# Turned keys and queries fetched chunk by chunk, and running sums of logs placed directly ahead of or within the second chunk's value products

## The chip, the cores and the metric

The kernel runs on one core of one Trainium2 chip. The metric is the device time of that core in microseconds; less is better. The engines that matter here are TensorE (PE: matrix products, results in PSUM), VectorE (DVE), ScalarE (ACT) and SyncE (SP), which issues most of the DMAs. Each engine executes its own instructions strictly in the order in which they stand in its program.

## The reference

Attention with a complex gate, followed by a two-layer MLP whose activation is h·cos(h). B=4 sequences, H=8 heads, S=768 steps, D=48; the MLP is 384 → 2048 → 384 on 3072 tokens. All in float32.

```python
mag = np.sqrt(a_re * a_re + a_im * a_im)
scale = np.minimum(mag, 0.999) / (mag + 1e-06)
a_re_n, a_im_n = (a_re * scale, a_im * scale)
for t in range(S):
    new_re = ar * S_re - ai * S_im          # ar, ai: step t of the gate
    new_im = ar * S_im + ai * S_re
    S_re, S_im = (new_re + outer(k[t], v[t]), new_im)
    y[:, :, t] = q[t] @ S_re
...
x = y.transpose(0, 2, 1, 3).reshape(B * S, H * D)
h = x @ w_in
out = (h * np.cos(h)) @ w_out
```

The kernel doesn't step through t. Since the gate multiplies, the state at step t is a sum over earlier steps s with weight P(t)/P(s), where P is the running product of the complex gate. So keys are divided by P and queries multiplied by it (written as real vectors of 96 = 2 x 48 numbers), and within a chunk of steps the result is a masked matrix product. The running product comes from logs: its magnitude is the exponential of a running sum of the log of the magnitude, its phase a running sum of angles.

## The kernel before

**Tiling.** The 3072 (sequence, step) rows are cut into 24 chunks of 128 steps, six to a sequence. Two chunks make a group; there are 12 groups, 0 to 11. The main loop runs over groups 2 to 11; below, **pass n** is its turn for group n. Groups 0 and 1 go through a start-up part ahead of it.

**What a pass does.** Pass n carries three groups at once:

- Group n, attention. For each of its two chunks: `sc` (scores, `f_scores`, L1021: 8 heads, keys `kT` against queries `qT`, in two halves of four heads), which DVE masks into `atm`; `sp` (`state_sums`, L1090, called by `f_state`: keys `ks` against values `v`, what the chunk adds to the running state; it is left out in the last chunk of a sequence, which is the second chunk of passes 2, 5, 8 and 11); `yp` (value products, `f_out`, L1036: four pairs of heads, p = 0 to 3, each with two products of `atm` with `v` and two of `qT` with `state`). ACT copies `yp` to `yT` (two copies for each chunk). "First scores" and "second scores" of a chunk pair are those of its first and its second chunk. After both chunks `yT` is sent to DRAM as `x` (`f_x`, L1118) and fetched back in another layout as `xT` (`f_xt`, L1127).
- Group n, first layer. `xT` times `w_in` gives `hp` (part of the columns by three products of split numbers: `xx`, `xh`, `xl`, the cross product being `hb`); `gate` is `hp` times its cosine. Group n-1, second layer: seven products of blocks, `sum` and `op`, with `t_...` and `w_out` against sums of `gate`; their result `ot` goes out. These fill PE between the steps of attention.
- Group n+1, the gate. ACT and DVE work out the log of the magnitude, `lg`, and split it into two halves, `hi` (ACT, L733) and `lo` (DVE). PE sums them along the steps: `lgs` (`p_powers`, L822: for each of two chunks one product with `hi` and one with `lo`, four matmuls in all, in two PSUM tiles). ACT takes four exponentials of `lgs` (P and 1/P), loads another table, and takes the arctangent of the angle. The angle is split and summed in the same way: `phs` (`g_phase`, L928). Sine and cosine of that, times P, turn keys and queries (`ks`, `qs`, `g_stack`, L963). DVE then transposes them in 32x32 blocks (`tr`, in `f_transpose`, L978), SP sends them to a DRAM buffer `moved` (one for keys, one for queries), and fetches them from there as `kT` and `qT`, with 96 numbers on the partitions and the steps along the free axis, as `sc` of the next pass wants them.

The tiles `kT` and `qT` exist once each, and so does `yT`. PSUM tiles of `sc`, `sp`, `yp`, `lgs` and `phs` come from one pool of five buffers (`pa`).

**What sets the order.** The body of a pass is one call of `weave`. It takes lists of steps, each with two numbers lo and hi between 0 and 1, spreads a list's steps evenly from lo to hi, sorts all by position, and calls them. For PE that order is final. So it is for the DMAs on SP's queue: `behind` adds an order without a wait between two of them. DVE and ACT are ordered by a scheduler that looks at what each step depends on. The row that matters here is `(prods(n + 1), 0.2285, 0.2315)`: the two `p_powers` calls of the next group, at those positions. `(chunks(n), 0.0, 0.36)` holds, for chunk after chunk, two calls of `f_scores`, `f_state` and `f_out`.

```python
def prods(g):                                              # L1458
    return powers(g) if 0 <= g < NG else []
...
for n in range(g * G, g * G + G):                          # L1483, chunks(g)
    for hh in range(2):
        yield lambda n=n, hh=hh: f_scores(n, hh)
    yield lambda n=n: f_state(n)
    yield lambda n=n: f_out(n)
```

**The fetch of turned keys and queries.** In the main loop `f_transpose` is called with both chunks at once, first for `kT`, then for `qT`. The call for `kT` only sends. The call for `qT` sends the queries and then issues four key fetches, one for each quarter of the steps of a chunk (q4, 32 steps), each with both chunks and all heads, and then two query fetches, one for each chunk. The loads and stores that `turned_first` and `rest_of` (L1501, L1506) put on the queue come behind the last query fetch.

Of the kernel before, what the change touches and what calls it, by code (L numbers as in the profile page):

```python
# [487 lines left out]
def fast_path(ctx, tc, q, k, v, a_re, a_im, moe_w_in, moe_w_out, out, least, odd, wide,  # L488
# [7 lines left out]
    nc = tc.nc  # L496
    B, H, S, D = q.shape
    DM, DF = moe_w_in.shape
    C = 128
    NCH = S // C  # L500
    G = 2
# [5 lines left out]
    Q4 = C // 32  # L507
# [26 lines left out]
    late = {}  # L534
# [8 lines left out]
    def behind(ins, other):  # L543
        tc.add_manual_dep(ins.ins, other.ins.name, mybir.DependencyInfo(
            mybir.DependencyClass.NoSync, mybir.DependencyReason.DATA))
# [14 lines left out]
    X = [dict() for _ in range(NG)]  # L560
# [130 lines left out]
    def matmul(out, **kw):  # L691
        chain(nc.tensor.matmul(out, **kw), "tensor")  # L692
# [193 lines left out]
    def p_even(g, i, n):  # L886
        for _ in even_steps(g, i, n):
            pass
# [10 lines left out]
    def p_apply(g, i, n):  # L899
        x = X[g]  # L900
        P, Q, u = (cut(x[name], i, n) for name in ("P", "Q", "mag"))
        x["applied"] = vector.tensor_tensor(out=Q, in0=cut(x["k"], i, n), in1=Q, op=ALU.mult)
        if g > PEG:
            return lambda: vector.tensor_tensor(out=u, in0=cut(x["q"], i, n), in1=P, op=ALU.mult)
        vector.tensor_tensor(out=u, in0=cut(x["q"], i, n), in1=P, op=ALU.mult)

    def g_angle(g, i, n):

        at = cut(X[g]["tan"], i, n)
        special(out=at, in_=at, func=AF.Arctan)  # L910
# [4 lines left out]
    def g_carry(g):  # L915

        n, some = g * G, ds(C - 32, 32)
        if g >= PEG and n % NCH:
            head = cut(X[g]["tan"], 0, 1)[some]
            X[g]["carried"] = vector.scalar_tensor_tensor(  # L920
                out=head, in0=before(n)[some], scalar=carry[some], in1=head,
                op0=ALU.mult, op1=ALU.add)

    def g_split(g):
        if g >= PEG:
            X[g]["split"] = upper_half(g, cut(X[g]["tan"], 0, G), 1.0 / math.pi)()
# [51 lines left out]
    def f_transpose(g, i, n, name):  # L978


        tr = ft.tile([C, NB, n * H, 32], F32, tag=name, name="tr", bufs=1)
        turn = vector.transpose(out=tr, in_=X[g][name[0] + "s"][:, ds(i * H, n * H)].rearrange(
            "p x a d -> p x (a d)").rearrange("p x (r b) -> p b x r", b=NB))
        X[g][name + " turn"] = turn
        if g and name == AHEAD and "apart" in X[g - 1]:
            behind(turn, X[g - 1]["apart"])
        elif g and "apart" in X[g - 1]:
            behind(turn, X[g - 1]["product"])
        moved = rows_d.tile([Q4, D2, n * H, 32], F32, tag="moved", name="moved", bufs=3)
        put = nc.sync.dma_start(out=moved.rearrange("q (r b) x j -> (q r) b x j", b=NB), in_=tr)  # L990
        behind(put, late.get("ends", late["x"]))
        X[g][name] = ft.tile([D2, G * H, Q4, 32] if name == "kT" else [D2, G, Q4, H, 32], F32,
                             tag=name, name=name, bufs=1)
        if name == "kT":
            X[g]["moved keys"] = moved
        else:
            for q4 in range(Q4):
                behind(nc.sync.dma_start(out=X[g]["kT"][:, ds(i * H, n * H), q4],
                                         in_=X[g]["moved keys"][q4]), put)
            for i_ in range(n):  # L1000
                late["qT"] = nc.sync.dma_start(
                    out=X[g][name][:, i_], in_=moved[:, :, ds(i_ * H, H)].rearrange("q c x j -> c q x j"))

    def f_turn(g, i, name, hh):

# [9 lines left out]
    def queries(n, h):  # L1015
        g, i = divmod(n, G)
        if g < PEG:
            return X[g]["qT"][:, i * H + h].rearrange("p q j -> p (q j)")
        return X[g]["qT"][:, i, :, h]
# [13 lines left out]
        if "whole" in X[n // G - 1]:  # L1033
            behind(y["masked"], X[n // G - 1]["whole"])

    def f_out(n):  # L1036
        y, (g, i) = Y[n], divmod(n, G)
        vals = X[g]["v"][:, i]
        state = y.get("state")
        if i == 0:  # L1040
            X[g]["yT"] = ft.tile([C, HH, G, C], F32, tag="yT", name="yT", bufs=1)
        ps = pa.tile([C, HH, C], F32, tag="a", name="yp")
        for p in range(HH):
            for side in range(2):
                matmul(ps[ds(side * 64, D), p], lhsT=vals[:, 2 * p + side],
                       rhs=y["atm"][:, 2 * p + side], start=True, stop=(state is None))
            if state is not None:
                for side in range(2):
                    matmul(ps[ds(side * 64, D), p], lhsT=state[:, 2 * p + side],
                           rhs=queries(n, 2 * p + side), start=False, stop=True)  # L1050
        for side in range(2):
            half = ds(side * 64, D)
            copied = scalar.copy(out=X[g]["yT"][half, :, i], in_=ps[half])
            if g >= PEG:
                behind(copied, late["upper"])
# [399 lines left out]
    def powers(g):  # L1455
        return [lambda i=i: p_powers(g, i) for i in range(G)]

    def prods(g):  # L1458
        return powers(g) if 0 <= g < NG else []

    def carries(g):
        if not 0 <= g < NG:
            return
        yield lambda: g_angle(g, 0, G)
        if g <= PEG:
            yield lambda: (g_carry(g), g_split(g))
            yield lambda: (p_even(g, 0, G), p_apply(g, 0, G))
        else:
            yield lambda: p_around(g)
# [4 lines left out]
    def angles(g):  # L1474
        if g < NG:
            yield lambda: g_rest(g)
        if g + 1 < NG:
            yield lambda: load(g + 1, ("re",))
# [4 lines left out]
    def chunks(g):  # L1483
        for n in range(g * G, g * G + G):
            for hh in range(2):
                yield lambda n=n, hh=hh: f_scores(n, hh)
            yield lambda n=n: f_state(n)
            yield lambda n=n: f_out(n)
        yield lambda: (f_x(g), g + 2 < NG and load(g + 2, ("im",), put=after_x), f_xt(g))
        if PEG < g + 1 < NG:  # L1490
            yield lambda: (ends(g + 1), load(g + 1, ("v",), put=lambda **kw: behind(
                nc.sync.dma_start(**kw), late["ends"])))
        if g + 2 < NG:
            late["next"] = [lambda: load(g + 2, ("k", "q"), put=turned_first)]
# [23 lines left out]
    def second(g, i):  # L1518
        return [lambda j0=j0: mm2(g, i, j0, 4) for j0 in range(0, NJ, 4)] if g < PLAIN else []
# [289 lines left out]
    for n in range(2, NG):  # L1809
        turned_keys, plain = list(keys(n + 1)), n == PLAIN  # L1810
        split = x_halves(n) if any(three(n, jp) for jp in THREE) else ()
        guard_ = list(guarded(("kT", "qT"))) if n > 2 else []
        convert = [lambda jp=jp: halves(jp) for jp in THREE if FROM[jp] == n + 1]
        weave((mixes(n - 1, 2, 4), 0.0, 0.08), (logs(n + 1), 0.0, 0.02), (chunks(n), 0.0, 0.36),
              (upper[2:] if plain else [], 0.0, 0.2), (products(n - 1, 0, 1), -0.02, -0.01),
              (products(n - 1, 1, 2), 0.05, 0.24), (products(n - 1, 2, 3) if n < NG - 1 else [], 0.28, 0.36),
              (mixes_again(n - 1, "s3"), 0.06, 0.18), (mixes_again(n - 1, "s2"), 0.19, 0.27),
              (angles(n + 1), 0.2695, 0.2699), (prods(n + 1), 0.2285, 0.2315), (carries(n + 1), 0.336, 0.34), (second(n - 1, 1), 0.36, 0.5),
              (mixes_again(n - 1, "s4"), 0.37, 0.48),
              (products(n - 1, 2 + (n < NG - 1), 7), 0.4, 0.56),  # L1820
              (convert[0:-2], 0.76, 0.76), (convert[-2:], 0.76, 0.98),
              (phases(n + 1), *((0.472, 0.476) if plain else (0.476, 0.484))),
              (turned_keys[0:1], 0.5, 0.5), (split[0:1], *[0.54 if n < NG - 1 else 0.525] * 2), (turned_keys[1:2], 0.53, 0.53),
              (turned_keys[2:3], 0.56, 0.56), (turned_keys[3:4], 0.6, 0.6), ([lambda: rest_of(n - 1)], 0.605, 0.605), (split[1:2], *[0.542 if n < NG - 1 else 0.53] * 2),
              (split[2:3], *[0.544 if n < NG - 1 else 0.54] * 2), ([lambda: p_end(n + 1, 0, G)] if n + 1 < NG else [], 0.615, 0.615), (last_quarter() if plain else [], 0.9, 1.0), (first(n), 0.56, 1.0),
              (mixes(n, 0, 2), 0.98 if convert else 0.92, 1.0 if n < NG - 1 else 0.97), (guard_[0:1], 0.47, 0.47),
              (guard_[1:2], 0.505, 0.505))
# [102 lines left out]
```

## Time and profile before

| | us |
|---|---|
| three timed runs | 638.99, 636.96, 638.65 |
| median | 638.65 |
| the profiled execution | 638.96 |
| its span | 637.2 |

The profile describes one execution. Busy time of an engine is the sum of its instructions; the groups of instructions that the profile lists by line, engine and tile show what it was spent on. The five costliest groups on PE are `hp` from `xT` (104.8 us in 492 matmuls), `op` (102.9 in 464), `hp` from `xh` (60.2 in 342) and from `xl` (59.0 in 342), and `sum` (52.5 in 304). `sc` takes 50.0 us in 384; the heaviest group of ACT is `gate` from `hp` (67.2 us in 96), that of DVE `gate` from `hp` (39.1 in 57). A float32 matmul stands as two records in the trace, so the 8 products of `sp` are 16 there.

Most matmuls have the same line, 692, a helper through which all of them go; they are told apart by their tiles, written out<-in. A line also shows the number of records (x16) and, in square brackets, what the first of them waited for: the time, the engine and tile that released it. SPq is the DMA queue of SP: a row there is a DMA being issued, not its transfer.

The granted clock of PE was 0.997 of full speed over the span, and the DMA queues moved 94.97 MB in it.

### The profile page before, as it was taken

The page shows a single profiled execution, that of the slowest core. Times are in us where ns is not written, and L with a number is a line of the kernel's source. Part 1 is how long each engine was busy: PE and PEld are TensorE (multiplying, and loading weights), DVE is VectorE, ACT ScalarE, POOL GpSimd, SP SyncE. Part 2 cuts the span into 40 slices and gives each one's busy share as a digit, 9 for nine tenths or more (in the row PEclk, how much of TensorE's full clock was granted, in tenths as well). Part 3 has the DMA queues.
Part 4 walks back from the last instruction along what each step waited for, and adds up shares of the span by engine and source line. Part 5 has one row for each costly group of instructions (what it writes and reads, how often), then busy time and mean ns, then how long its engine had stood idle before and what let it go on. Part 6 is the DMA issues. An engine that isn't in the chain of part 4 may idle for free.

```text
span 637.2 us, 11706 instructions
## 1 busy us (share of the span) xinstructions
PE 618.9 (97%) x4417; PEld 569.8 (89%) x4417; DVE 543.8 (85%) x878; ACT 463.0 (73%) x832; POOL 28.5 (4%) x45
## 2 busy tenths in 40 slices
PE   8999999999999999999999999999999999999996
PEld 5788868677889989998999999999999999989996
DVE  6999989888898798899999999989989989983471
ACT  7888687294697596698698697598598598661450
POOL 4010110000000000000000000000000000000000
PEclk9999999999999998999999999999999999999999
DMA  9968564725926647476486486496496494371001
GB/s 235 242 193 224 182 188 82 204 53 113 248 65 159 167 109 198 133 166 174 136 189 173 125 200 168 107 223 170 115 214 170 103 224 126 99 174 50 26 2 32
DMA packets 236926, 94.97 MB, mean 149 GB/s; under 512 B 208862, under 2 KB 229087, under 8 KB 236859
## 3 DMA queue, kind: packets, MB, share of 16 engines
q1 hardware_dynamic: 229320, 68.51, 46.1%
q0 software_dynamic: 5824, 25.50, 12.5%
q8 instruction: 37, 0.61, 0.4%
q10 hardware_dynamic: 1714, 0.11, 0.2%
q14 instruction: 31, 0.25, 0.1%
HBM read 69.28 MB, written 24.81 MB: 148 GB/s over the span
## 4 chain that ended last, share of the span: by engine, by line
PE 70%; ACT 14%; DVE 8%; DMA 4%; issue 3%; SPq 0%; ACTq 0%; DVEq 0%
PE hp L692 20%; PE op L692 16%; PE sum L692 13%; PE yp L692 5%; PE sc L692 5%; PE sp L692 3%; PE hb L692 3%; DMA qT<-moved 3%; PE phs L692 2%; ACT xT L681 2%; ACT gate L712 2%; DVE tr L681 2%; ACT rs L712 1%; DVE ks L681 1%; ACT tan L712 1%
## 5 line engine op out<-in xcount | busy, mean ns | idle before, releaser
L692 PE MATMUL hp<-xT,w_in 128*128 128x256 f32 (+1 forms) x492 | 104.8, 369 | 0.0
L692 PE MATMUL op<-w_out,gate 128*128 128x192 f32 (+1 forms) x464 | 102.9, 372 | 0.0
L692 PEld LDWEIGHTS hp<-xT,w_in 128*128 128x128 f32 x492 | 89.7, 190 | 12.6 <-issue 0.2
L712 ACT ACTIVATE gate<-hp,half_pi_b 128x512 f32<-128x512 f32 x96 | 67.2, 701 | 41.1 <-PE hp L692 22.4
L692 PEld LDWEIGHTS op<-w_out,gate 128*128 128x128 f32 x464 | 78.7, 190 | 15.2 <-issue 0.4
L692 PE MATMUL hp<-xh,wh 128*128 128x256 f32 x342 | 60.2, 285 | 0.0
L692 PE MATMUL hp<-xl,wl 128*128 128x256 f32 x342 | 59.0, 281 | 0.0
L681 ACT ACTIVATE xT<-hp 128x512 bf16<-128x512 f32 x96 | 58.5, 609 | 0.0
L692 PE MATMUL sc<-qT,kT 96*128 96x128 f32 x384 | 50.0, 279 | 2.6 <-DMA qT<-moved 2.3
L692 PEld LDWEIGHTS sc<-qT,kT 96*128 96x128 f32 x384 | 46.4, 191 | 6.8 <-issue 4.2
L692 PE MATMUL sum<-w_out,gate 128*128 128x192 f32 x304 | 52.5, 326 | 0.0
L692 PEld LDWEIGHTS hp<-xh,wh 128*128 128x128 f32 x342 | 48.9, 188 | 1.5 <-ACT xh L681 1.4
L692 PEld LDWEIGHTS sum<-w_out,gate 128*128 128x128 f32 x304 | 49.5, 190 | 0.1
L692 PE MATMUL hb<-xx,wx 128*128 128x256 f32 x342 | 48.6, 282 | 0.0
L692 PEld LDWEIGHTS hp<-xl,wl 128*128 128x128 f32 x342 | 48.4, 188 | 0.0
L681 DVE SCALAR_TENSOR_TENSOR gate<-hp,gate 128x512 f32<-128x512 f32 x57 | 39.1, 685 | 9.9 <-ACT xT L681 9.9
L681 ACT ACTIVATE gate<-hb 128x512 f32<-128x512 f32 x57 | 35.7, 626 | 13.0 <-PE hb L692 11.9
L681 DVE TENSOR_TENSOR hp<-hp,gate 128x512 f32<-128x512 f32 x57 | 39.2, 693 | 6.7 <-PE hp L692 2.6
L692 PEld LDWEIGHTS hb<-xx,wx 128*128 128x128 f32 x342 | 44.0, 188 | 0.0
L681 ACT ACTIVATE ot<-sum 128x192 f32<-128x192 f32 x39 | 12.8, 329 | 38.4 <-PE sum L692 35.6
L681 DVE TENSOR_TENSOR atm<-sc,causal 128x512 f32<-128x512 f32 x48 | 32.2, 682 | 7.3 <-PE sc L692 6.9
L681 ACT COPY yT<-yp 48x512 f32<-48x512 f32 x44 | 25.4, 577 | 17.0 <-PE yp L692 16.3
(162 smaller groups left out, 1286.0 us busy)
## 6 DMA issues: line engine op xcount, KB each, us to landing
moved<-tr SPq DMA_DIRECT2D x20, 768.0 KB
raw<-in_moe_w_in_dram POOLq DMA_DIRECT2D x16, 768.0 KB, 6.1
raw<-in_moe_w_out_dram POOLq DMA_DIRECT2D x16, 768.0 KB, 5.2
kT<-moved SPq DMA_DIRECT2D x40, 192.0 KB
qT<-moved SPq DMA_DIRECT2D x20, 384.0 KB
k<-in_k_dram SPq DMA_DIRECT2D x24, 192.0 KB
q<-in_q_dram SPq DMA_DIRECT2D x24, 192.0 KB
v<-in_v_dram SPq DMA_DIRECT2D x24, 192.0 KB
```

The source lines that it names most:

```text
L681: ins = getattr(self.engine, op)(**kw)
L692: chain(nc.tensor.matmul(out, **kw), "tensor")
L712: chain(nc.scalar.activation(func=func, **kw))
```

## The change

It has two parts.

**The fetch.** In place of four key fetches with both chunks and then two query fetches, it is now, for the first chunk, four key fetches of half the size and the query fetch of that chunk, and then the same for the second chunk. Each is ordered behind the one ahead of it. The bytes are the same; the number of DMAs in a pass goes from six to ten.

**The sums of logs.** `prods(n + 1)` leaves the table of the pass. `f_out` gets a function `between` and calls it ahead of its first pair of heads, or ahead of its third (p = 2) in the last chunk of a sequence. `chunks` passes `prods(g + 1)` in for the second chunk of a group.

```diff
--- before.py
+++ after.py
@@ -994,12 +994,15 @@
         if name == "kT":
             X[g]["moved keys"] = moved
         else:
-            for q4 in range(Q4):
-                behind(nc.sync.dma_start(out=X[g]["kT"][:, ds(i * H, n * H), q4],
-                                         in_=X[g]["moved keys"][q4]), put)
             for i_ in range(n):
-                late["qT"] = nc.sync.dma_start(
-                    out=X[g][name][:, i_], in_=moved[:, :, ds(i_ * H, H)].rearrange("q c x j -> c q x j"))
+                part = ds(i_ * H, H)
+                for q4 in range(Q4):
+                    home = nc.sync.dma_start(out=X[g]["kT"][:, part, q4],
+                                             in_=X[g]["moved keys"][q4, :, part])
+                    behind(home, put)
+                put = late["qT"] = nc.sync.dma_start(
+                    out=X[g][name][:, i_], in_=moved[:, :, part].rearrange("q c x j -> c q x j"))
+                behind(put, home)
 
     def f_turn(g, i, name, hh):
 
@@ -1033,7 +1036,7 @@
         if "whole" in X[n // G - 1]:
             behind(y["masked"], X[n // G - 1]["whole"])
 
-    def f_out(n):
+    def f_out(n, between=lambda: None):
         y, (g, i) = Y[n], divmod(n, G)
         vals = X[g]["v"][:, i]
         state = y.get("state")
@@ -1041,6 +1044,8 @@
             X[g]["yT"] = ft.tile([C, HH, G, C], F32, tag="yT", name="yT", bufs=1)
         ps = pa.tile([C, HH, C], F32, tag="a", name="yp")
         for p in range(HH):
+            if p == (0 if n % NCH < NCH - 1 else 2):
+                between()
             for side in range(2):
                 matmul(ps[ds(side * 64, D), p], lhsT=vals[:, 2 * p + side],
                        rhs=y["atm"][:, 2 * p + side], start=True, stop=(state is None))
@@ -1485,7 +1490,7 @@
             for hh in range(2):
                 yield lambda n=n, hh=hh: f_scores(n, hh)
             yield lambda n=n: f_state(n)
-            yield lambda n=n: f_out(n)
+            yield lambda n=n: f_out(n, lambda: n % G and [t() for t in prods(g + 1)])
         yield lambda: (f_x(g), g + 2 < NG and load(g + 2, ("im",), put=after_x), f_xt(g))
         if PEG < g + 1 < NG:
             yield lambda: (ends(g + 1), load(g + 1, ("v",), put=lambda **kw: behind(
@@ -1815,7 +1820,7 @@
               (upper[2:] if plain else [], 0.0, 0.2), (products(n - 1, 0, 1), -0.02, -0.01),
               (products(n - 1, 1, 2), 0.05, 0.24), (products(n - 1, 2, 3) if n < NG - 1 else [], 0.28, 0.36),
               (mixes_again(n - 1, "s3"), 0.06, 0.18), (mixes_again(n - 1, "s2"), 0.19, 0.27),
-              (angles(n + 1), 0.2695, 0.2699), (prods(n + 1), 0.2285, 0.2315), (carries(n + 1), 0.336, 0.34), (second(n - 1, 1), 0.36, 0.5),
+              (angles(n + 1), 0.2695, 0.2699), (carries(n + 1), 0.336, 0.34), (second(n - 1, 1), 0.36, 0.5),
               (mixes_again(n - 1, "s4"), 0.37, 0.48),
               (products(n - 1, 2 + (n < NG - 1), 7), 0.4, 0.56),
               (convert[0:-2], 0.76, 0.76), (convert[-2:], 0.76, 0.98),
```

What the change moves on PE, in pass 3, where the second chunk isn't the last of its sequence. The rows start at the second half of the second scores; a row is a line, an operation, out<-in, the shape of one and how many in a row. Before:

```order
L692 MATMUL sc<-qT,kT 128x128 x4
L692 MATMUL lgs<-hi,exact 128x384
L692 MATMUL lgs<-lo,exact 128x384
L692 MATMUL lgs<-hi,exact 128x384
L692 MATMUL lgs<-lo,exact 128x384
L692 MATMUL sp<-v,ks 96x48 x8
L692 MATMUL yp<-atm,v 48x128 x2
```

PE in pass 3 after the change:

```order
L692 MATMUL sc<-qT,kT 128x128 x4
L692 MATMUL sp<-v,ks 96x48 x8
L692 MATMUL lgs<-hi,exact 128x384
L692 MATMUL lgs<-lo,exact 128x384
L692 MATMUL lgs<-hi,exact 128x384
L692 MATMUL lgs<-lo,exact 128x384
L692 MATMUL yp<-atm,v 48x128 x2
```

The four sums have gone behind the eight products of `sp`; the rest of these rows stands as it did.

PE in pass 5, where the second chunk is the last of its sequence and has no `sp`. Before:

```order
L692 MATMUL sc<-qT,kT 128x128 x4
L692 MATMUL lgs<-hi,exact 128x384
L692 MATMUL lgs<-lo,exact 128x384
L692 MATMUL lgs<-hi,exact 128x384
L692 MATMUL lgs<-lo,exact 128x384
L692 MATMUL yp<-atm,v 48x128 x2
L692 MATMUL yp<-qT,state 48x128 x2
L692 MATMUL yp<-atm,v 48x128 x2
L692 MATMUL yp<-qT,state 48x128 x2
L692 MATMUL yp<-atm,v 48x128 x2
```

PE in pass 5 after the change:

```order
L692 MATMUL sc<-qT,kT 128x128 x4
L692 MATMUL yp<-atm,v 48x128 x2
L692 MATMUL yp<-qT,state 48x128 x2
L692 MATMUL yp<-atm,v 48x128 x2
L692 MATMUL yp<-qT,state 48x128 x2
L692 MATMUL lgs<-hi,exact 128x384
L692 MATMUL lgs<-lo,exact 128x384
L692 MATMUL lgs<-hi,exact 128x384
L692 MATMUL lgs<-lo,exact 128x384
L692 MATMUL yp<-atm,v 48x128 x2
```

Here the sums have gone behind the first two pairs of heads of `yp`. The other passes are as one of these two: 4, 6, 7, 9 and 10 as pass 3, 2 and 8 as pass 5; pass 11 has no next group and no sums.

SP's queue at the place in a pass where the turned queries are sent and fetched (`tr` is the transposed tile, `moved` the DRAM buffer, `ot` a result of the second layer). Before:

```order
L990 DMA moved<-tr 128x1536 x2
L998 DMA kT<-moved 96x16x32 x4
L1001 DMA qT<-moved 96x4x256 x2
L1502 DMA out_dram<-ot 128x384 x2
```

SP's queue at the same place after the change (the new lines shift the numbers: L998 is L1000, L1001 is L1003, L1502 is L1507):

```order
L990 DMA moved<-tr 128x1536 x2
L1000 DMA kT<-moved 96x8x32 x4
L1003 DMA qT<-moved 96x4x256
L1000 DMA kT<-moved 96x8x32 x4
L1003 DMA qT<-moved 96x4x256
L1507 DMA out_dram<-ot 128x384 x2
```

The first chunk's queries stand ahead of the second chunk's keys, and the stores behind have four more DMAs ahead of them. On ACT the order is the same, but that a table load stands behind the two copies of `yT` in passes 2 and 8, where it stood ahead of them. On DVE a few steps of the state and of the end of the running product change places with steps of the gate, and the transposing of the queries stands one or two gate steps later in one or two passes.

## Prediction

> **What bounds the kernel now.** The page comes first: its busy times and the shares of the chain that ended last.
>
> ```profile
> span 637.2 us, 11706 instructions
> PE 618.9 (97%) x4417; PEld 569.8 (89%) x4417; DVE 543.8 (85%) x878; ACT 463.0 (73%) x832; POOL 28.5 (4%) x45
> PE 70%; ACT 14%; DVE 8%; DMA 4%; issue 3%; SPq 0%; ACTq 0%; DVEq 0%
> ```
>
> TensorE (PE) works 97% of the span and carries 70% of the chain. VectorE (DVE), the next engine, has 15% of room. So a change that adds and removes no arithmetic can only gain where PE stands still, and the second view is the list of what PE waited for.
>
> ```profile
> PE lgs L692 <- DVE lo L681: 3.0, 5, 0.8
> PE sc L692 <- DMA qT<-moved: 2.3, 3, 1.5
> PE lgs L692 <- ACT hi L733: 2.0, 4, 0.8
> ```
>
> The columns are total us, times, longest. These are the three largest waits of the main loop. Two of them belong to the running sums of logs (`lgs`, 5.0 us in nine waits), one to the scores (`sc`) at the head of a pass, which wait for turned keys and queries (2.3 us in three). The change touches these two places and no other.
>
> The timeline of PE gives the true price of a wait. A row reads start, length, line, out<-in, count of weight loads and matmuls. First pass 7, where `lgs` waits for nothing, then pass 6, where it waits twice.
>
> ```profile
> 385.79 1.06 PE L692 MATMUL sc<-qT,kT 96*128 96x128 f32 x8
> 386.60 0.42 PE L692 MATMUL lgs<-hi,exact 128*128 128x384 f32 x1
> 386.86 0.34 PE L692 MATMUL lgs<-lo,exact 128*128 128x384 f32 x1
> 387.38 1.48 PE L692 MATMUL sp<-v,ks 128*96 128x48 f32 x16
> 388.79 0.43 PE L692 MATMUL yp<-atm,v 128*48 128x128 f32 x4
> 390.69 0.59 PE L692 MATMUL sum<-t_s,gate 128*128 128x192 f32 x2
> ```
> ```profile
> 335.64 1.06 PE L692 MATMUL sc<-qT,kT 96*128 96x128 f32 x8
> 336.91 0.44 PE L692 MATMUL lgs<-hi,exact 128*128 128x384 f32 x1 [0.21 <-ACT hi L733]
> 337.90 0.45 PE L692 MATMUL lgs<-lo,exact 128*128 128x384 f32 x1 [0.56 <-DVE lo L681]
> 338.54 1.48 PE L692 MATMUL sp<-v,ks 128*96 128x48 f32 x16
> ```
>
> From the start of the second scores to the start of `sp` pass 7 takes 387.38 - 385.79 = 1.59 us, pass 6 takes 338.54 - 335.64 = 2.90. The two waits cost 1.31 us, while the brackets add up to 0.77: each break in the stream costs 0.27 more than its bracket. For nine waits that is 5.0 + 9 x 0.27 = **7.4 us**.
>
> **The change, part one: what stands in front of `lgs`.** Nothing is added or removed; four `lgs` matmuls move behind `sp`, or in the last chunk of a sequence behind half of `yp`. From pass 7: `sp` lasts 388.79 - 387.38 = 1.41 us, `yp` 390.69 - 388.79 = 1.90, so half of it 0.95, and `lgs` starts 0.81 after the second scores. In passes 6 and 9 `sp` covers the whole wait: in pass 6 `lgs` would start at 335.64 + 0.81 + 1.41 = 337.86; its second matmul comes 386.86 - 386.60 = 0.26 later and finds `lo` there (337.90). In passes 3, 4 and 5 something stays:
>
> ```profile
> 184.24 1.06 PE L692 MATMUL sc<-qT,kT 96*128 96x128 f32 x8
> 186.95 0.45 PE L692 MATMUL lgs<-lo,exact 128*128 128x384 f32 x1 [0.83 <-DVE lo L681]
> ...
> 235.75 1.06 PE L692 MATMUL sc<-qT,kT 96*128 96x128 f32 x8
> 238.57 0.44 PE L692 MATMUL lgs<-lo,exact 128*128 128x384 f32 x1 [0.56 <-DVE lo L681]
> ...
> 288.08 1.06 PE L692 MATMUL sc<-qT,kT 96*128 96x128 f32 x8
> 290.74 0.45 PE L692 MATMUL lgs<-lo,exact 128*128 128x384 f32 x1 [0.55 <-DVE lo L681]
> ```
>
> Pass 3 would ask for `lo` at 184.24 + 0.81 + 1.41 + 0.26 = 186.72 and gets it at 186.95; pass 4 at 238.23 and 238.57; pass 5, with only 0.95 in front, at 290.10 and 290.74. With 0.27 for each break that leaves 0.5 + 0.6 + 0.9 = 2.0 us. **Part one is worth 7.4 - 2.0 = 5.4 us.** Its ends: 7.4 if all of it were covered; 0 if the sums turn out to wait as long behind `sp`, for a PSUM bank that ACT has to empty first.
>
> What is moved late by this: in passes 7, 8 and 10, which wait for nothing today, the sums come 0.95 to 1.41 us later, and with them four exponentials, a table load and the copies of `yT` on ACT, then the way of `x` through DRAM to the first `hp`.
>
> ```profile
> 388.89 1.28 ACT L708 ACT_TABLE_LOAD   x1
> 390.81 0.58 ACT L681 COPY yT<-yp 48x512 f32<-48x512 f32 x1 [0.64 <-PE yp L692]
> ...
> 301.86 0.38 SPq L1132 DMA_DIRECT2D xT<-x  x1
> ...
> 307.51 1.67 PE L692 MATMUL hp<-xT,w_in 128*128 128x256 f32 x7
> ...
> 586.15 0.38 SPq L1132 DMA_DIRECT2D xT<-x  x1
> ...
> 589.48 0.56 DVE L681 TENSOR_SCALAR cut<-xT 128x768 uint32<-128x768 uint32 x1 [1.28 <-DMA xT<-x]
> ```
>
> In pass 7 the table load ends 0.64 before `yp` is done; 1.41 later it would hold `yT` up by 0.77. The last row pair says that `xT` is there 589.48 - 586.15 = 3.3 us after its issue (DVE was waiting for it), and the pass with the least room, pass 5, has 307.51 - 301.86 = 5.65. So 2.3 us of cover lie over 0.77, or over the 0.8 by which PE gets ahead in pass 5. I count this delay at nothing; without that cover it costs 0.8 us in each of nine passes, 7 us.
>
> **Part two: keys and queries chunk by chunk.** The same bytes in 8 key transfers of half size instead of 4, and the first chunk's queries after four of them. The case that waits longest is pass 11.
>
> ```profile
> 325.17 2.76 PE L692 MATMUL sum<-w_out,gate 128*128 128x192 f32 x16
> 327.77 1.50 PE L692 MATMUL sc<-qT,kT 96*128 96x128 f32 x12
> ...
> 566.36 2.76 PE L692 MATMUL sum<-w_out,gate 128*128 128x192 f32 x16
> 570.63 2.02 PE L692 MATMUL sc<-qT,kT 96*128 96x128 f32 x16 [1.51 <-DMA qT<-moved]
> 577.10 1.16 PE L692 MATMUL sc<-qT,kT 96*128 96x128 f32 x8
> ```
> ```profile
> 557.91 6.31 SPq L998 DMA_DIRECT2D kT<-moved  x4
> 564.40 1.68 SPq L1001 DMA_DIRECT2D qT<-moved  x2
> ```
> ```profile
> L998 SPq DMA_DIRECT2D kT<-moved x40: 584/1260/3012, 114.0 to 563.4; - x40
> ```
>
> Pass 6 shows the pace without a wait: scores 2.60 us after the last `sum`. Pass 11 takes 4.27, so its wait costs 1.67, or 0.16 more than its bracket. For three waits: 2.3 + 3 x 0.16 = **2.8 us**.
>
> Do these go? A key transfer holds the queue for 0.58 to 3.0 us at one size (last row, least, median, most), so most of that is waiting for room and should follow the amount. The trace has no half transfer. Bounds: half the pass-11 mean, 0.79, or all of it, 1.58. I take 0.79, since 0.58 without a jam for a whole one lies below it. Then the first chunk is issued by 557.91 + 4 x 0.79 + 0.84 = 561.9 instead of 565.2, and if it lands 5.4 us later as now (570.63 - 565.24), at 567.3, before PE wants it at 566.36 + 2.60 = 568.96. Even 1.2 us each would do. The second chunk's issue ends where it does now and is wanted at 577.10 - 1.67 = 575.4. The stores and loads behind it on the queue keep their time, and above 0.79 wait with it. **Part two: 2.8 us; ends 0 and 3.1** (a few tenths in passes 8 and 10 are not in the list).
>
> **A third term: the clock.** In pass 4 the granted clock falls to half right after the two `lgs` waits.
>
> ```profile
> 239.20 1.76 PE L692 MATMUL sp<-v,ks 128*96 128x48 f32 x16
> ...
> 244.10 2.87 PE L692 MATMUL sum<-t_s,gate 128*128 128x192 f32 x16
> ```
> ```profile
> 241.00:243.00 2.00, 2.00 (x20) 1.98 (x22) 2.00 (x4) 1.49 (x2) 0.00 (x0) 0.50 0.92 224
> ```
>
> The third number from the right is the clock: 0.50. From `sp` to `sum` pass 4 takes 4.90 us, pass 7 390.69 - 387.38 = 3.31: the stretch costs **1.6 us**. It is the only one in the loop, and it begins some 2 us after PE stood for 239.20 - 235.75 - 1.59 = 1.86 us at the two sums. Of the three timed runs one is 1.7 to 2.0 us below the others, which looks like a run without it. With two thirds of that wait gone (0.6 stays) I expect the stretch gone too.
>
> The Trainium skill, "TensorE: Matmul & The Clock Gate", part 1, puts the fall to half clock behind at least one idle window of about 3.4 us. No gap here is that long, so by that rule these waits do not cause the stretch, and it would stay; the trace, with half clock after shorter gaps, does not bear the rule out, but it is one event.
>
> **The sum.** The profiled execution took 638.96 us (span 637.2 and 1.76 around it), 0.3 above the median of 638.65. 638.96 - 5.4 - 2.8 - 1.6 = **629.2 us**.
>
> **Rivals.** *The clock stretch stays, or falls elsewhere*: 638.96 - 8.2 = 630.8. For it: a single event in the loop, not seen after the 1.3 us of pass 6.
>
> *Part two brings nothing*, since the first chunk lands no earlier: half transfers at over 1.2 us. 638.96 - 5.4 - 1.6 = 632.0. Against it: 0.58 for a whole one.
>
> *The late exponentials hold up `xT`*, without the cover: 629.2 + 7 = 636. Against it: the 2.3 us; part of it is likelier than all.
>
> *Slower: a transfer has a price of its own.* If a half key transfer holds the queue as long as a whole one, 1.58, the second chunk of pass 11 is issued by 557.91 + 8 x 1.58 + 1.68 = 572.2 and lands at 577.6, 2.2 after PE wants it. In nine passes that is 20 us, with part two lost: 638.96 + 20 - 7.0 = 652. It decides from (575.4 - 5.4 - 1.68 - 557.91) / 8 = 1.3 us each. For it: the median of 1.26 is near. Against it: the least of 0.58.
>
> The Trainium skill, "DMA: Bandwidth & Descriptors", anatomy of one DMA, gives every transfer about 2.0 us fixed plus bytes / 436e3, and its rules tell authors to merge small ones; four more transfers in series would be an estimated 8 us later. The trace has whole ones at a mean of 1.58, below that fixed part alone, so they overlap.
>
> *Waits only move*, to `lo` of the phase sums or a gate: about 638, for no row shows where.
>
> **How the numbers follow.** Forecast 0.42, clock stays 0.20, part two nothing 0.12, `xT` 0.12, slower 0.06, waits only move 0.08. A measurement here tells some 0.3%, 1.9 us, from no change. Faster: the first three and most of the fourth, 0.83; same 0.11; slower 0.06. Range: low end with all of part one, 3.1 and the clock, 638.96 - 12.1 = 626.9; the high end takes in 632.0 and the milder part of the `xT` case, 635.5.
>
> **What would show it.** PE's list of waits: no `sc` behind `qT`, `lgs` at 1 us or so, in three passes. The key rows of the queue: near 0.8 us each, 6.3 for eight. The clock at 1.00 from 238 to 246. Wrong would be: `hp` or `phs` in that list, second scores waiting for `qT`, or `lgs` waiting as long as before.

## The result and the profile after

| | before | after |
|---|---|---|
| four timed runs, median | 637.81 us (636.74 to 638.99) | 631.48 us (631.48 to 631.77) |
| ratio | | 0.9902, 95% interval 0.9879 to 0.9924 |
| profiled execution | 638.96 us, span 637.2 | 631.48 us, span 629.6 |

The change makes the kernel faster by 1.0%. In the experiments below two runs stand far outside all others (2387.1 and 1059.3 us) and are left out of the counts; they move a median by less than 0.1 us. Execution against execution that is 7.5 us, where the forecast had 9.8. The page of the changed kernel, its busy times and its chain:

```profile
span 629.6 us, 11793 instructions
PE 617.2 (98%) x4417; PEld 567.4 (90%) x4417; DVE 542.8 (86%) x878; ACT 462.9 (74%) x832; POOL 28.6 (5%) x45
PE 87%; ACT 6%; DVE 2%; DMA 2%; SPq 1%; issue 1%; ACTq 0%; DVEq 0%
```

PE now carries 87% of the chain instead of 70. PE's list of waits in the main loop:

```profile
PE sum L692 <- ACT ot L681: 1.4, 2, 1.1
PE yp L692 <- DVE atm L681: 0.3, 1, 0.3
PE lgs L692 <- DVE lo L681: 0.2, 1, 0.2
```

All three waits of before are gone or nearly so (2.3 us behind `qT`, 5.0 us at `lgs`). A new one has come, and it is the largest: a sum of the second layer behind ScalarE's copy `ot`.

The list doesn't say what this is worth. That comes from the starts of rows in PE's timeline, pass by pass, in us. A is from the first scores to the last start in the second chunk's `yp`, B from there to `phs`, C from the last `sum` to the next pass's scores.

| pass | A before | A after | B before | B after | C before | C after |
|---|---|---|---|---|---|---|
| 2 | 14.52 | 14.86 | 7.87 | 7.87 | 2.60 | 2.60 |
| 3 | 14.20 | 12.89 | 8.09 | 8.08 | 2.59 | 2.60 |
| 4 | 16.79 | 13.87 | 8.09 | 9.48 | 2.60 | 2.60 |
| 5 | 13.72 | 12.98 | 8.09 | 8.59 | 2.60 | 2.60 |
| 6 | 13.75 | 12.53 | 8.09 | 8.33 | 3.30 | 2.60 |
| 7 | 13.42 | 13.42 | 8.09 | 8.08 | 2.73 | 2.60 |
| 8 | 12.10 | 12.36 | 8.09 | 8.09 | 3.00 | 2.60 |
| 9 | 13.35 | 12.52 | 8.09 | 8.34 | 2.83 | 2.60 |
| 10 | 13.41 | 13.41 | 8.09 | 8.09 | 4.27 | 2.60 |

C gives back 3.13 us: the scores wait nowhere. A gives back 1.31, 0.74, 1.22 and 0.83 in passes 3, 5, 6 and 9, and 2.92 in pass 4, of which some 1.6 is the stretch of half clock. Against that stand two losses: 0.34 and 0.26 in A of passes 2 and 8, where the sums now break the value products, and 1.39 + 0.50 + 0.24 + 0.25 = 2.4 us in B of passes 4, 5, 6 and 9.

Pass 4 shows where B's loss comes from. First come rows of PE in the changed kernel (start, length, line, out<-in, records, and in brackets the wait), then rows of ScalarE from the same stretch.

```profile
235.52 1.48 PE L692 MATMUL sp<-v,ks 128*96 128x48 f32 x16
236.82 0.42 PE L692 MATMUL lgs<-hi,exact 128*128 128x384 f32 x1
237.42 0.44 PE L692 MATMUL lgs<-lo,exact 128*128 128x384 f32 x1 [0.18 <-DVE lo L681]
...
240.04 2.87 PE L692 MATMUL sum<-t_s,gate 128*128 128x192 f32 x16
242.75 2.76 PE L692 MATMUL op<-t_a,gate 128*128 128x192 f32 x16
246.64 2.87 PE L692 MATMUL sum<-t_s,s 128*128 128x192 f32 x16 [1.13 <-ACT ot L681]
249.21 0.47 PE L692 MATMUL phs<-hi,exact 128*128 128x384 f32 x1
```
```profile
243.54 0.84 ACT L712 ACTIVATE tan<-tan 128x768 f32<-128x768 f32 x1 [0.98 <-DVE tan L681]
245.39 0.84 ACT L733 ACTIVATE hi<-tan 128x768 fp32r<-128x768 f32 x1 [1.01 <-DVE tan L681]
246.26 0.33 ACT L681 ACTIVATE ot<-sum 128x192 f32<-128x192 f32 x1
```

The second layer's `sum` collects four products in one PSUM buffer, and each partial result is copied out (`ot`) before the next is added. The copy in question could run from 242.9 on, when the first `sum` row ends. It runs at 246.26, since it stands in ScalarE's order behind `hi<-tan`, the split of the angle, and that waits for VectorE. So PE stands until 246.64. Before, ScalarE had the same order, but PE came to the same row later and the copy was done:

```profile
247.52 0.84 ACT L733 ACTIVATE hi<-tan 128x768 fp32r<-128x768 f32 x1 [1.01 <-DVE tan L681]
248.38 0.33 ACT L681 ACTIVATE ot<-sum 128x192 f32<-128x192 f32 x1
249.41 2.76 PE L692 MATMUL sum<-t_s,s 128*128 128x192 f32 x16
```

The new wait takes the place of the one removed.

The clock and the key fetch in the changed kernel: a window row (the third number from the right is the granted clock) and the row of the key DMAs (least, median, most ns).

```profile
240.00:242.00 2.00, 2.00 (x15) 1.96 (x13) 2.00 (x4) 1.95 (x4) 0.75 (x1) 1.00 0.87 213
L1000 SPq DMA_DIRECT2D kT<-moved x80: 320/612/2762, 113.9 to 559.2; - x80
```

No window of the loop shows half clock any more, and a half transfer holds the queue for about half of what a whole one does (584 and 1260 ns, least and median).

### The profile page after: what moved, and what is told of

Read it like the earlier page. It is cut to its first block, busy times and chain, and to the rows that moved or that the text cites. A ratio compares the mean times of both kernels' runs of the same rounds, so it can differ in the third digit from the quotient of the medians.

```text
span 629.6 us, 11793 instructions
## 1 busy us (share of the span) xinstructions
PE 617.2 (98%) x4417; PEld 567.4 (90%) x4417; DVE 542.8 (86%) x878; ACT 462.9 (74%) x832; POOL 28.6 (5%) x45
## 4 chain that ended last, share of the span: by engine, by line
PE 87%; ACT 6%; DVE 2%; DMA 2%; SPq 1%; issue 1%; ACTq 0%; DVEq 0%
PE hp L692 28%; PE op L692 18%; PE sum L692 15%; PE sc L692 6%; PE hb L692 6%; PE yp L692 5%; PE sp L692 3%; PE phs L692 2%; PE lgs L692 1%; ACT tan L712 1%; PE yr L692 1%; ACT L708 1%; PE tp L1014 1%; ACT lg L712 1%; ACT rs L712 1%
## 5 line engine op out<-in xcount | busy, mean ns | idle before, releaser
L681 DVE TENSOR_TENSOR gate<-hp,gate 128x512 f32<-128x512 f32 x39 | 26.3, 680 | 12.3 <-ACT xT L681 12.1
```

Source lines behind the costliest of these rows:

```text
L681: ins = getattr(self.engine, op)(**kw)
```

## The experiments

Times are medians of the runs, and each ratio is against runs of before on the same chip.

### Each part alone

Only the sums: the changed kernel with the six-DMA fetch of before put back.

```diff
+            for q4 in range(Q4):
+                behind(nc.sync.dma_start(out=X[g]["kT"][:, ds(i * H, n * H), q4], ...), put)
             for i_ in range(n):
-                part = ds(i_ * H, H)
...
+                late["qT"] = nc.sync.dma_start(out=X[g][name][:, i_], ...)
```

> Only the sums of logs moved, the fetch as before. In the changed kernel's trace the waits at the sums are gone (5.4 us), two passes lose 0.6 us to a break inside the value products, and 2.4 us of new waits stand in front of the second layer's sum (behind the copy ot on ScalarE) in passes 4, 5, 6 and 9. Theory A, the two parts add up: 631.48 + 3.1 = 634.6 us, the same four new waits, no stretch of half clock near 240 us and so times within 0.5 us of each other. Rival B, the sums gain only because keys and queries come early too: over 636 us. Rival C, the new waits come from the earlier fetch alone: they are missing here and the time is 632.2.

Measured: 636.00 us (635.32 to 637.46), ratio 0.9945 (0.9917 to 0.9973). PE's waits:

```profile
PE sc L692 <- DMA qT<-moved: 2.9, 3, 1.2
PE sum L692 <- ACT ot L681: 1.4, 2, 1.2
PE sc L692 <- ACT gate L712: 0.9, 1, 0.9
```

The new wait is there without the new fetch in passes 4, 5 and 6 (B = 9.52, 8.59 and 8.31), so rival C falls. In pass 9, whose scores come late here, it is missing (B = 8.10). The scores wait longer than in before: interval C of passes 6, 8, 9 and 10 is 3.69, 3.94, 3.61 and 3.59, together 4.4 us over 2.60, against 3.1. PE, put ahead at the sums, arrives at `qT` earlier, and `qT` comes no sooner. Theory A (634.6) misses by about that 1.3 us; the truth lies between A and B.

Only the fetch: the kernel before with the ten-DMA fetch.

> Only the fetch changed, the sums of logs as before. Theory A, the two parts add up: the 3.1 us in front of the scores are gone and the waits at the sums stay as they are; 636.8 - 3.1 = 633.7 us in runs without the stretch of half clock in pass 4, 635.6 in runs with it, and both kinds occur, as in the four timed runs of before (636.74, 636.96 and 638.65, 638.99). Rival B, PE comes earlier to sums that are no earlier, and waits there for what it saved at the scores in passes 7 to 10 (1.46 us; pass 11 has no sums and keeps its 1.67): 635.1 and 637.0, with waits at lgs in passes 7, 8 or 10 that before has not.

Measured: 636.5 us (634.94 to 641.89), ratio 0.9971 (0.9943 to 0.9999). The scores wait nowhere. The sums wait as in before, 4.7 us in the list and in the same passes, so rival B's waits in passes 7, 8 and 10 don't appear. Pass 4 has 0.77 at `ot` (B = 8.86) that didn't show in before, where half clock held PE back. Pass 9's sums wait 0.32 longer. These 1.1 us are most of the difference between the least disturbed runs, 634.94, and the 633.7 of theory A. In this trace pass 4 keeps its full clock, but pass 3 doesn't. Two window rows of it:

```profile
187.00:188.00 1.00, 1.00 (x10) 0.99 (x11) 1.00 (x3) 0.98 (x4) 0.00 (x0) 1.00 0.79 156
189.00:190.00 1.00, 1.00 (x10) 0.90 (x11) 0.68 (x2) 0.98 (x2) 0.00 (x0) 0.50 0.97 323
```

So the stretch isn't tied to one pass; in both traces it follows long waits at the sums. The two medians alone gain 2.8 and 2.3 us; each part hands some of its gain to a wait that the other removes.

### The new wait

One number pair of the pass's table is shifted, so that the copy is written between the arctangent and the split; PE's order stays the same.

```diff
-... (products(n - 1, 2, 3) if n < NG - 1 else [], 0.28, 0.36), ...
+... (products(n - 1, 2, 3) if n < NG - 1 else [], 0.278, 0.358), ...
```

> The changed kernel, with one copy of the second layer (ot of its fourth product, out of the PSUM bank that the sum accumulates in) placed on ScalarE ahead of the split of the angle (hi<-tan) instead of behind it. Theory A, the new waits of the sum are a matter of that order: the split waits for VectorE's angle and the copy stands behind it; with the copy ahead, 2.4 us go: 629.1 us, and no sum behind ot in PE's list. Rival B, ScalarE and VectorE have become the bound there: the wait moves to the phase sums (phs behind hi or lo), 631 to 631.5 us.

Measured: 629.03 us (628.81 to 629.27), ratio 0.9844 (0.9804 to 0.9883). ScalarE in pass 4, then PE:

```profile
243.99 0.84 ACT L712 ACTIVATE tan<-tan 128x768 f32<-128x768 f32 x1 [0.99 <-DVE tan L681]
244.85 0.33 ACT L681 ACTIVATE ot<-sum 128x192 f32<-128x192 f32 x1
245.84 0.85 ACT L733 ACTIVATE hi<-tan 128x768 fp32r<-128x768 f32 x1 [0.66 <-DVE tan L681]
```
```profile
240.48 2.87 PE L692 MATMUL sum<-t_s,gate 128*128 128x192 f32 x16
243.19 2.76 PE L692 MATMUL op<-t_a,gate 128*128 128x192 f32 x16
245.79 2.76 PE L692 MATMUL sum<-t_s,s 128*128 128x192 f32 x16
248.25 0.47 PE L692 MATMUL phs<-hi,exact 128*128 128x384 f32 x1
```

The copy uses time in which ScalarE stood waiting for VectorE. B is 8.09 again in passes 4, 5, 6 and 9, the 2.4 us are back, and `phs` doesn't wait in their place. Theory A holds: it was the order on ScalarE, not its or VectorE's load.

### The place within the value products

The changed kernel with the sums in front of the value products in every pass (`p == 0`).

> The changed kernel, with the sums of logs in front of the value products in every pass, so also in passes 2, 5 and 8. Theory A: a break inside the value products costs 0.3 us, so passes 2 and 8, which never waited, gain 0.34 + 0.26 = 0.6; pass 5 gets its wait at the sums back, of which the changed kernel had kept only 0.24 in the end, since 0.5 came back as a wait at the second layer's sum: 631.48 - 0.6 + 0.24 = 631.1 us. Rival B: the place within the products is worth what it saves at the sums in pass 5 (0.74) and the 0.6 is something else: 631.5 to 632.2.

Measured: 631.49 us (630.82 to 631.91). PE's waits show the trade in pass 5: the sums wait again (0.6 behind `hi`, 0.6 behind `lo`) and one wait behind `ot` goes.

```profile
PE sum L692 <- ACT ot L681: 1.1, 1, 1.1
PE lgs L692 <- DVE lo L681: 0.7, 2, 0.6
PE lgs L692 <- ACT hi L733: 0.6, 1, 0.6
```

A is 14.52 and 12.21 in passes 2 and 8 (0.34 and 0.15 less), 13.71 in pass 5 (0.73 more, of which B gives back 0.50). The profiled executions take 631.48 both; the runs can't tell the two theories apart. The place is nearly neutral, as long as the copy is late.

With the copy ahead, and the sums within the value products in pass 5 alone (`p == (2 if g == 5 else 0)`):

> The copy ahead of the split, and the sums within the value products in pass 5 alone (in passes 2 and 8 in front of them). By the segments of the runs so far the break costs 0.34 us in pass 2 and 0.15 in pass 8, and pass 5 keeps its 0.73: theory A 629.03 - 0.5 = 628.5 us. Rival B, the break in pass 8 only hides a wait that then shows elsewhere: 628.9 to 629.1.

Measured: 628.72 us (628.43 to 629.01), ratio 0.9830 (0.9797 to 0.9863), the quickest kernel of the study but for one below that is its equal. Interval A is 0.34 and 0.16 shorter in passes 2 and 8, about as forecast; that the total of 629.03 and 628.72, taken on two chips, differs by 0.3 is within what these runs can tell.

### The stretch of half clock

All of these have the new fetch and the copy ahead. First the sums back at their old place in passes 3, 4 and 5 only.

```diff
-yield lambda n=n: f_out(n, lambda: n % G and ...)
+yield lambda n=n: f_out(n, lambda: g not in (3, 4, 5) and n % G and ...)
...
+(prods(n + 1) if n in (3, 4, 5) else [], 0.2285, 0.2315),
```

> The copy ahead of the split, but the sums of logs at their old place in passes 3, 4 and 5, the three with the longest waits (1.75, 1.86 and 1.69 us before). Both theories bring the waits back: 1.31 + 1.33 + 0.73 = 3.4 us, 632.4. Theory W, those waits cause the stretch of half clock (in pass 4 before, in pass 3 with only the fetch changed): 1.6 to 2 us more in part of the runs, so that they spread over 632 to 634.5. Rival S, the stretch comes with the chip or with the waits at the scores, which are gone here: all runs within 0.6 us around 632.4.

Measured: 632.99 us, six runs: 632.54, 632.60, 632.73, 633.26, 633.45 and 637.12, the last at a mean clock of 0.992 where the others have 0.997 or 0.998. The waits come back as forecast (A = 14.19, 15.19 and 13.73). One run of six is far off; that decides nothing.

The same in passes 6 and 9, whose waits are shorter:

> The copy ahead of the split, but the sums of logs at their old place in passes 6 and 9, whose waits are shorter (1.31 and 0.83 us before). Waits back: 629.03 + 1.2 + 0.8 = 631.0 us. Theory W with a limit between 1.3 and 1.7 us of wait: no stretch, runs within 0.6 us. Rival: any wait at the sums brings the stretch, some runs at 632.7.

Measured: 631.39 us (631.19 to 632.50), mean clocks 0.998 and 0.999. A is 1.19 and 1.16 longer in the two passes; no sign of a stretch.

The old place in passes 3, 4 and 5, with 20 matmuls of 128 columns ahead of the first sum:

> As the run with the old place in passes 3, 4 and 5, but with 20 small matmuls in front of the first sum in those passes, whose result the sums overwrite, so that PE works where it stood (an estimated 1.5 us of work). Theory W, standing still causes the stretch: no stretch in any run, all within 0.6 us, at 632.4 to 633. Rival S, the stretch has nothing to do with PE standing still: the same spread as the run without the fill.

Measured: 634.69 us. The fill was too long by 0.4 to 0.5 us a pass (A = 14.69, 15.58 and 14.26). The profiled execution has no stretch in the loop, but of the eleven runs that count three have a mean clock below 0.997, one of them 639.36 us at 0.993. Work in place of standing still didn't remove the low clocks.

Then a pair that differs in the place of the sums in passes 3, 4 and 5 and in nothing else, on one chip. All sums at the old place (in the text on record, 9 of 12 for the run with only the fetch is a miscount; it is 7 of 12):

> The fetch of the change and the copy ahead of the split, all sums of logs at their old place. Waits at the sums back in passes 3, 4, 5, 6 and 9: 628.7 + 1.31 + 1.33 + 0.73 + 1.2 + 1.2 = 634.5 us. Theory W, the waits in passes 3 to 5 cause the stretch of half clock: as in the run with only the fetch changed (where 9 of 12 runs had a mean clock below 0.997, and the profiled one a stretch in pass 3), half of the runs or more have a mean clock of 0.996 or less and take 636 us. Rival S: mean clocks as in the next run.

> The same, but the sums of logs at the new place in passes 3, 4 and 5 alone. Waits at the sums in passes 6 and 9 only: 628.7 + 2.4 = 631.1 us, 3.4 less than the run above where neither has a stretch. Theory W: no run with a mean clock below 0.997. Rival S: as many as in the run above.

Measured: all old, 637.70 us; four runs at 634.6 to 634.9 with clocks of 0.998, three at 637.7 with 0.994 or 0.995, four from 640.8 to 643.8 with 0.986 to 0.989. New place in passes 3 to 5, 631.44 us, six runs from 631.04 to 632.16, all at 0.998 or 0.999. The profiled execution of the first is one of the long ones (641.29 us); its windows in passes 3 and 4, then one window of the second kernel:

```profile
188.00:190.00 2.00, 2.00 (x17) 1.91 (x17) 1.22 (x2) 1.98 (x4) 0.00 (x0) 0.50 0.95 328
190.00:192.00 2.00, 2.00 (x22) 1.98 (x20) 2.00 (x4) 0.42 (x1) 0.00 (x0) 0.50 0.81 161
...
244.00:246.00 2.00, 2.00 (x20) 1.90 (x20) 1.42 (x4) 1.50 (x2) 0.00 (x0) 0.50 0.88 222
246.00:248.00 2.00, 2.00 (x20) 1.68 (x16) 2.00 (x4) 0.00 (x0) 0.00 (x0) 0.50 0.47 92
```
```profile
188.00:190.00 2.00, 2.00 (x33) 1.81 (x28) 2.00 (x5) 1.98 (x5) 0.14 (x1) 1.00 0.98 348
```

Undisturbed, the pair differs by 634.6 - 631.4 = 3.2 us, the waits; with stretches by 6 and more. Seven of eleven runs against none of six: with the old place in passes 3 to 5 the half clock comes, so theory W holds as far as the place goes. All changed kernels of this document, on several chips, say the same: with the sums at the new place in these passes 1 of 55 runs has a mean clock below 0.997, with the old place 15 of 29 (the fill not counted). The one is in the next section, 638.42 us at 0.993, with long waits at the scores, so the old place isn't the only way to it. Why it comes in some runs only, and whether it is the standing still, stays open: the fill speaks against it, and the profiled execution of the run with the old place in passes 3, 4 and 5 had these waits and no stretch.

### The fetch, with the copy ahead

The quickest kernel with the fetch of before:

> The quickest kernel so far (copy ahead of the split, the sums within the value products in pass 5 alone) with the fetch of before: four whole key fetches and then both queries. Theory A, the fetch is worth 3 us by itself wherever PE stands: 628.7 + 3.1 = 631.8 us. Rival B, the fetch is worth more once PE comes earlier: the waits at the scores were 4.4 us in the run with only the sums moved, and 2.4 us of waits at the sum are now gone too, so that PE comes earlier still: 633 us or more. Either way these waits should bring back a spread of 1 us and more between runs, against 0.6.

Measured: 633.68 us (632.07 to 638.42). Its waits:

```profile
PE sc L692 <- DMA qT<-moved: 3.9, 4, 1.3
PE sc L692 <- ACT xT L681: 0.4, 1, 0.4
```

C adds up to 1.33 + 0.92 + 1.42 + 0.85 + 0.53 = 5.05 us over 2.60, and 628.7 + 5.05 is 633.75. (The kernel of the next run, on the same chip, took 628.71.) Rival B holds: the same fetch is worth 3.1 us to the kernel before and 5.0 to a PE that waits for nothing else. The spread is back as well, with one run of six at 638.42 us and a mean clock of 0.993.

The quickest kernel with keys in sixteen transfers:

```diff
+for h2 in range(2):
+    some = ds(i_ * H + h2 * HH, HH)
+    home = nc.sync.dma_start(out=X[g]["kT"][:, some, q4], in_=X[g]["moved keys"][q4, :, some])
+    behind(home, put)
...
```

> The same quickest kernel with keys in quarters: sixteen transfers of four heads in a pass instead of eight of eight heads. Theory A, a key transfer holds the queue by its amount (least and median of whole ones 584 and 1260 ns, of halves 320 and 612): quarters near 0.3 us at the median, no wait at the scores, 628.7 us. Rival B, a transfer has a price of its own: the means of whole ones and halves, 1.27 and 0.85, lie on a line with 0.43 for each transfer and 0.84 for a whole one's amount, so a quarter takes 0.64, eight of them 5.1 instead of 3.4, and the first chunk comes 1.7 us later, of which the waits at the scores show 0.5 to 1.5 in each of five or more passes: 632 to 636 us.

Measured: 628.71 us (628.27 to 629.31). The row of its key transfers:

```profile
L1002 SPq DMA_DIRECT2D kT<-moved x160: 312/477/1718, 113.8 to 559.0; - x160
```

The truth of the queue lies between the theories: a quarter has a least of 312 ns, no less than a half's 320, so the least doesn't follow the amount any more, and the median of 477 is well above half of 612. But it costs nothing here: no scores wait, and the time is that of the eight transfers.

## Why the prediction was right in its sign and too large in its size

- **The waits at the sums** were forecast at 7.4 us, of which 2.0 stay. The table has 1.31 + 0.74 + 1.22 + 0.83, and in pass 4 2.92 less 1.6: 5.4 us, the number of the text. The method, starts of rows instead of the brackets in the list, gave it.
- **What is late by this** is the step that failed. The text went along the exponentials and `yT` to `xT`, found cover there, and put the delay at nothing. That path was indeed covered: no `hp` waits. But the cost came up on another edge, PE waiting for the PSUM buffer of `sum`, which ScalarE's copy empties, behind the split of the angle. It is 2.4 us in four passes. The rival "waits only move" named the phase sums and the gate, and "no row shows where"; the row was there, the copy behind `hi<-tan` in ScalarE's timeline. The run with the copy ahead shows cause and size.
- **The break in the value products** was not in the sum. It costs 0.34 and 0.26 us in passes 2 and 8, which had no wait to remove.
- **Keys and queries**: forecast 2.8, its upper end 3.1, measured 3.13. A half transfer was taken at 0.79; in pass 11 the first four take 4.64 us of queue, 1.16 each, more than that and just under the 1.2 which the text gave as sufficient; the second four take 0.82 each. The slower rival, decided from 1.3 us each, was nearer in that pass than the median of 612 ns suggests. Even sixteen transfers didn't reach it: they hold the queue for 5.24 + 4.13 = 9.37 us there, and eight at 1.3 would be 10.4. What the prediction takes from the Trainium skill, "DMA: Bandwidth & Descriptors", as 2.0 us for every transfer, the section on the anatomy of one DMA gives for DMAs issued by GpSimd; these are issued by SyncE. Four more of them in a pass cost PE nothing here: C is 2.60 throughout.

The queue in pass 11 of the changed kernel:

```profile
552.25 4.64 SPq L1000 DMA_DIRECT2D kT<-moved  x4
557.11 0.37 SPq L1003 DMA_DIRECT2D qT<-moved  x1
557.52 3.29 SPq L1000 DMA_DIRECT2D kT<-moved  x4
560.85 0.53 SPq L1003 DMA_DIRECT2D qT<-moved  x1
```

- **The clock**: 1.6 us were counted, and the stretch is gone from the profiled execution. That its place depends on the sums in passes 3 to 5 is shown by the pair of runs; that PE's standing still causes it was the text's argument and is not shown. The term also was that of one execution: two of the four timed runs of before, at 636.74 and 636.96, look like runs without it, so the median gains less than the profiled execution did. That the forecast started from an execution with a stretch was luck for this term.
- **The parts were added up** as if they were independent. With nothing else changed they gain 2.8 and 2.3 us, together with the removal of each other's waits more.

The balance: 638.96 - 5.4 + 0.6 + 2.4 - 3.1 - 1.6 = 631.9, against 631.48; the remaining 0.4 lies ahead of pass 2 (0.16 us earlier) and in pass 11 and the end. The forecast of 629.2 lacked the 0.6 and the 2.4; the 0.3 more at the scores and this 0.4 made up for some, and what is left is the miss of 2.3 us.

The Trainium skill, "TensorE: Matmul & The Clock Gate", part 1, also says that the activity window is free-running. The traces agree: the stretch of before lasts 3.41 us, those of the run with all sums old 6.83 each, and the edges lie on a grid of 3.41 us (last section). Its condition, an idle window of about 3.4 us, isn't borne out: in the 3.41 us ahead of the fall in pass 4 of before, PE was busy for 2.11 us.

## What to carry to other kernels

When a wait on the busiest engine goes, ask of each later meeting of the engines which side used to be late, and read the other engine's order there: a small copy that frees a PSUM buffer behind an instruction that waits for a third engine is harmless until PE comes earlier. Price a wait by the starts of the rows around it in a pass with and in one without it. And don't add the gains of two edits that feed the same engine: each pays part of its gain into the other's wait, so that 2.8 and 2.3 us apart were 7.3 together in the kernel with the sums in front, run on the chip of those two.

## What the runs showed of the hardware that was not expected

Half clock comes in whole windows of one length. Read in steps of 0.1 us, the clock in the run with all sums at the old place falls and rises in these rows, and a mean between 0.50 and 1.00 tells where in the step:

```profile
188.00:188.10 0.10, 0.10 (x4) 0.10 (x2) 0.10 (x1) 0.10 (x1) 0.00 (x0) 0.51 0.47 164
194.80:194.90 0.10, 0.10 (x2) 0.10 (x2) 0.00 (x0) 0.10 (x1) 0.00 (x0) 0.86 0.95 184
242.60:242.70 0.10, 0.10 (x3) 0.10 (x3) 0.10 (x1) 0.10 (x1) 0.00 (x0) 0.57 0.83 164
249.40:249.50 0.10, 0.10 (x2) 0.10 (x2) 0.10 (x1) 0.10 (x1) 0.04 (x1) 0.80 0.00 0
```

So it falls at 188.00 and 242.61 and rises at 194.83 and 249.44. The distances are 6.83, 47.78 and 6.83 us, which is 2, 14 and 2 times 3.41. The stretch of before goes from 240.24 to 243.65, once 3.41, and that of the run with only the fetch from 188.42 to 191.84. The last fall of before, after PE's work, comes at 636.18, which is 392.53 us or 115 times 3.413 behind the rise. The edges thus lie on a grid that runs on by itself, and a stretch is one or two of its windows. A single one cost 1.6 us in before. A double one costs 3.2: A and B together are 25.49 and 26.48 in passes 3 and 4 of this run, and 22.28 and 23.28 in the run with the old place in passes 3, 4 and 5, which has no stretch. That is the step of about 3.1 us between most times of this kernel (634.6, 637.7, 640.8). What makes the clock fall isn't shown. In the window ahead of each of these four falls PE stood for 1.2 to 1.3 us; but in before it stood for 1.5 us of the window from 567.92 on, ahead of the scores of pass 11, and no fall followed.

A key transfer of half size held the queue for at least 320 ns and one of a quarter for 312, where a whole one has 584: below half size the least hold didn't shrink here.
